# Two score banks become one tile of two halves, with 1024-column exponentials in the last slot of a gated two-branch attention kernel

## The chip, the cores and the metric

The kernel runs on one core of a Trainium2 chip. The metric is the device time of one execution in microseconds (us). Engines in what follows: TensorE (PE; its weight loads are PEld), VectorE (DVE), ScalarE (ACT), GpSimd (POOL) and SyncE (SP), which issues most DMAs.

## The reference

Two attention branches over the same 2048 x 512 input, 32 heads of 16 columns, are mixed by a gate per row:

```python
g = _sigmoid((x * gate_w).sum(-1, keepdims=True))
a = _A_ref(x, A_wq, A_wk, A_wv, A_wo, A_beta)
b = _B_ref(x, B_wqkv, B_wo)
return g * a + (1 - g) * b
```

Branch B is plain softmax attention over all 2048 positions: `p = softmax(q k^T / 4)`, `o = p v`, then `o @ wo`. Branch A splits the sequence into four segments of 512. Inside a segment it is causal softmax attention; the earlier segments come in through a memory state, `num / den` with `phi(q)` and `phi(k)`, weighted by `sigmoid(beta)` per head. All values are float32.

## The kernel before, in words

**Start** (to about 350 us). The input is transposed and split into a high and a low part (`do_x`), and the projections are made as three products of such parts: `v_job` (L255) for V and `qk_job` (L274) for Q and K, twelve matmuls of 512 columns each into one PSUM bank, which ScalarE copies out and, for Q and K, VectorE reads too. `mem_out`, `mem_put`, `mem_tr` and `mem_upd` (L304 to L359) make the memory branch of A. Each of these takes a bank from `misc()` (L95), which gives the least recently used of the banks in `mode["misc"]`.

**Slots** (L905 to L939). 32 slots follow, k = 0 to 31. A slot handles four heads and 512 query columns of B (unit 32 + k) and of A (unit k). It has NG = 37 groups: 32 of B (16 key tiles, two pairs of heads) and 5 of A (L489). For a group, in this order:
- `t_group` (L491) takes two banks, multiplies K with Q into them (two matmuls of 64 rows by 512 columns, side by side in the array; a group of A has up to four narrower ones), and ScalarE takes the exponential of each bank into SBUF (`raw`, L509). For A, GpSimd then masks the diagonal blocks (L512).
- the planned tasks: `s_b` (L442) or `s_a` (L417), products in the other orientation whose row maxima VectorE takes out of the two-bank tiles `sbk`; they serve the softmax of the next slot. `m_chain` and `m_rows` (L455, L472) bring the maxima into rows of Q.
- `pvs` (L826): `pv` (L515) multiplies the exponentials of an earlier key tile with V into the bank `pvb`, 256 columns at a time (512 in the last slot); `fin_copy` (L528) copies the result out.
- `out_mm` (L587), in one group of each slot from k = 9, is half of an output tile's projection.

Nothing reorders this: the order of the calls is the order on each engine. Waits are added by the framework from the tiles that an instruction reads and writes.

**PSUM** has eight banks of 512 columns: tb0 and tb1 (`TB`, L82), `pvb`, `mb`, and two tiles `sbk` of two banks each. In the slots `t_group`, `m_rows` and `out_mm` draw from `T3`, that is tb0, tb1 and mb (L821), least recently used first (`bank`, L88). In slot 31 there are no maxima for a next slot, and the first halves of the two `sbk` tiles join the rotation (L907), five banks in all.

**Planning.** `spread` (L892) puts the 32 `s_b` tasks of a slot at groups 20 to 31 and 36 of the slot before and at groups 1 to 19 of the slot itself; the six `s_a` tasks (`ST_A`, L637) go to groups 32 to 36 and to group 0 of the next slot (L902).

**End** (L940 to L967). The last four output tiles are projected into the banks `TAIL` (L822), copied out in halves and stored.

Of the kernel before, what the change touches and what calls it, by code (L numbers as in the profile page):

```python
# [7 lines left out]
FT = mybir.dt.float32  # L8
# [3 lines left out]
AF = mybir.ActivationFunctionType  # L12
# [9 lines left out]
C = 512  # L22
NC4 = SEQ // C
NT = SEQ // 128
SCALE = 0.25
MASK = -4.0e9
EARLY = 6
S_FIRST = 10
S_LAST = 10
# [4 lines left out]
def gated_mix_kernel(ctx, tc, x, wq, wk, wv, wo, beta, wqkv, wob, gate_w, out):  # L34
    nc = tc.nc
# [5 lines left out]
    PS = ctx.enter_context(tc.tile_pool(name="ps", bufs=1, space=PSUM))  # L41
# [19 lines left out]
    PTILE = [RAW[:, 4 * n:4 * n + 4] for n in range(2)]  # L61
# [17 lines left out]
    aux = P.tile([E, 2, 64], FT, name="aux")  # L79
    MST = [[X.tile([128, 8, 32], FT, name=f"mst{i}{s}") for s in range(2)] for i in range(2)]  # L80

    TB = [PS.tile([128, C], FT, name=f"tb{i}") for i in range(2)]  # L82
    PVB = PS.tile([128, C], FT, name="pvb")
    MB = PS.tile([128, C], FT, name="mb")
    SBK = [PS.tile([128, 2, C], FT, name=f"sbk{i}") for i in range(2)]
    lru = []

    def bank(allowed):  # L88
        b = min(allowed, key=lambda a: max([n for n, x in enumerate(lru) if x is a], default=-1))
        lru[:] = [x for x in lru if x is not b] + [b]  # L90
        return b

    mode = {"misc": TB + [MB, PVB] + [b[:, 0] for b in SBK]}

# [14 lines left out]
    def rot(key, lst):  # L109
        i = cnt.get(key, 0)  # L110
        cnt[key] = i + 1
        return lst[i % len(lst)]
# [262 lines left out]
    def q_of(u):  # L375
        return QA[u % 2] if u < 32 else QB[u % 3]

    def k_of(u, p):
        return KA[u % 2][:, p] if u < 32 else KB[(u - 32) % 3][:, p]

    def load_q(u):
        kd, qd, c = UN[u]
        load_qk(q_of(u), kd, 0, qd, c)

    def load_ka(u):
        kd, qd, c = UN[u]
        load_qk(KA[u % 2], kd, 1, qd, c)

    def load_kb(k, c=None):
        dst = KB[k % 3] if c is None else KB[k % 3][:, :, c * C:(c + 1) * C]  # L390
        load_qk(dst, "B", 1, k % 8, c)
# [63 lines left out]
    def m_chain(k):  # L455
        mx = pair_max(k)
        if k == 1:
            nc.vector.memset(mx[:, 0], 0.0)
        if k < 32:
            nc.vector.tensor_reduce(mx[:, 1], MXB.pop(32 + k).rearrange("q j p i c -> q (j p) i c"), axis=AX.X,  # L460
                                    op=OP.max)
        else:
            nc.vector.memset(mx[:, 1], 0.0)
        del MX[k]
        mx = mx.rearrange("q u h i -> q (u h i)")
        m8 = M8[k] = W.tile([128, 2, 32], FT, name="m8")
        hi = W.tile([128, 32], FR, name="mhi")
        nc.vector.tensor_scalar(hi, mx, -1.0, None, op0=OP.mult)
        nc.vector.tensor_copy(m8[:, 0], hi)
        nc.vector.scalar_tensor_tensor(m8[:, 1], mx, -1.0, hi, op0=OP.mult, op1=OP.subtract)  # L470
# [20 lines left out]
    def t_group(u, n, banks):  # L491


        kd, qd, c = UN[u]
        bs = [bank(banks) for _ in range(2)]
        c0 = 0
        for it, hs in (((n // 2, (n % 2 * 2, n % 2 * 2 + 1)),) if kd == "B" else GA[n]):
            q0 = 128 * it if kd == "A" else 0
            w = C - q0
            pn = it if kd == "B" else it % 2  # L500
            for j, h in enumerate(hs):
                r = slice(64 * j, 64 * j + 64)
                nc.tensor.matmul(bs[j][:, c0:c0 + w], k_of(u, h // 2)[r, 128 * it:128 * it + 128],  # L503
                                 q_of(u)[r, h // 2, q0:], start=True, stop=True)
                PT[u, it, h] = PTILE[pn % 2][:, 2 + j if (kd, it) == ("A", 2) else h][:, c0:c0 + w]
            c0 += w
        for j in range(2):
            pt = PTILE[pn % 2][:, 2 + j if (kd, n) == ("A", 4) else hs[j]]
            nc.scalar.activation(pt, bs[j], AF.Exp, scale=SCALE)  # L509
            if kd == "A":  # L510
                m = pt[:, :128] if n < 2 else pt.rearrange("p (a t) -> p a t", a=4)[:, ::3 if n < 4 else 2]
                nc.gpsimd.affine_select(out=m, in_=m, pattern=[[1, 128]] if n < 2 else [[0, 2], [1, 128]],  # L512
                                        compare_op=OP.is_ge, fill=0.0, base=0, channel_multiplier=-1)
# [14 lines left out]
    def fin_copy(u):  # L528

        ps = W.tile([128, C], FT, name="pvs", bufs=1)  # L530
        if u < 31:
            nc.vector.tensor_copy(ps, PVB)
        else:
            nc.scalar.activation(ps, PVB, AF.Copy)  # L534
        AT["pd", u] = D.tile([4, 32, C], FT, name=f"pd{u}")
        nc.sync.dma_start(AT["pd", u].rearrange("h r t -> (h r) t"), ps)
# [77 lines left out]
    def tail_mm(t, gs, a):  # L614
        op = tail_ops(t)
        for g in gs:
            for oi, wi in TERMS:
                nc.tensor.matmul(TAIL[t], op[oi][:, g, a], (AT["wh"], AT["wl"])[wi][:, g, a],
                                 start=(oi, wi, g, a) == (0, 0, 0, 0), stop=(oi, wi, g, a) == (1, 0, 3, 0))

    def tail_out(t):
        tt = 12 + t
        for hf in range(2):
            yo = RAW[:, t + 4 * hf, :256]
            h = slice(256 * hf, 256 * hf + 256)
            if hf:
                nc.scalar.activation(yo, TAIL[t][:, h], AF.Copy)
            else:
                nc.vector.tensor_copy(yo, TAIL[t][:, h])
            nc.sync.dma_start(outr[tt * 128:(tt + 1) * 128, h], yo)  # L630


    def todo(fn, *a):
        return lambda: fn(*a)
# [87 lines left out]
    for blk in range(16):  # L722
        g, c = divmod(blk, 4)
        pg, pc = divmod(blk - 1, 4)
        if blk == 4:
            mode["misc"] = TB + [MB, PVB]
        if 4 <= blk < 14:
# [5 lines left out]
        n = blk + 1 + (c == 2)  # L733
# [39 lines left out]
        for n in range(3):  # L773
# [8 lines left out]
            if nf == 35:  # L782
                mode["misc"] = [MB, PVB, TB[1]]
            if nf < want:
# [34 lines left out]
            set_aux(KB[2][:, p], 0)  # L819

    T3 = TB + [MB]  # L821
    TAIL = T3 + [SBK[0][:, 0]]  # L822
    mode["misc"] = T3
    NG = 2 * NT + 5

    def pvs(k, n):  # L826

        ua, ub = k, 32 + k
        if n == 0:
            if k:  # L830
                pv(ua - 1, 2)
                fin_copy(ua - 1)
        elif k == 31 and n < 2 * NT:
            if n % 2 and n > 1:
                pv(ub, n // 2 - 1)
        elif 2 <= n < 2 * NT + 2:
            pv(ub, n // 2 - 1, n % 2 * 256, n % 2 * 256 + 256)
            if n == 2 * NT + 1:
                fin_copy(ub)
        elif n > 2 * NT + 1:  # L840
            m = n - 2 * NT - 2
            if m < 2:
                pv(ua, 0, 256 * m, 256 * m + 256)
            else:
                pv(ua, 1)
                pv(ua, 3)
# [43 lines left out]
    plan = {}  # L890

    def spread(tasks, gs):  # L892
        for n, p in enumerate(gs):
            plan.setdefault(p, []).extend(tasks[len(tasks) * n // len(gs):len(tasks) * (n + 1) // len(gs)])

    for k in range(31):
        if k:
            spread([todo(s_b, 33 + k, *t) for t in (sorted(ST_B, key=lambda t: t[2]) if k == 1 else ST_B)],
                   [(k - 1, n) for n in list(range(2 * S_FIRST, 2 * NT)) + [NG - 1]] + [(k, n) for n in range(1, 2 * S_LAST)])
        else:  # L900
            spread(st33[EARLY:], sorted([(0, n) for n in range(2 * S_LAST)] + [(0, 2 * n) for n in range(4)]))
        for n, t in enumerate(ST_A):  # L902
            plan.setdefault((k, 2 * NT + n) if n < 5 else (k + 1, 0), []).append(todo(s_a, k + 1, *t))

    for k in range(32):  # L905
        ua, ub = k, 32 + k
        banks = T3 + [b[:, 0] for b in SBK] * (k == 31)  # L907
        for n in range(NG):
            it = n // 2 if n < NG - 1 else NT + 2
            t_group(*(ub, n) if n < 2 * NT else (ua, n - 2 * NT), banks)  # L910
            for f in plan.get((k, n), []) + ex[k][0].get(n, []):
                f()
            pvs(k, n)
            for f in ex[k][1].get(n, []):
                f()
            if n % 2 == 0 and n < NG - 1:
                continue
            beside(k, it)
            if it == S_LAST:
                m_chain(k + 1)  # L920
            if it == 4 and not k:
                late()
            if it == 4 and not k:
                load_q(ub + 2)
                for c in range(NC4):
                    load_kb(2, c)
            if it == NT and k < 29:
                load_q(ub + 3)
                load_kb(k + 3)
            if it == 6 and k < 31:  # L930
                load_q(ua + 1)
                load_ka(ua + 1)
                if (ua + 1) % 2 == 0:
                    load_va(ua + 1)
            if it == 9:
                if k % 2 == 0 and k < 30:
                    load_vb(k // 2 + 1)
                if 1 <= k <= 4:
                    load_wo(k - 1)  # L939
# [55 lines left out]
```

## Time and profile before

| | us |
|---|---|
| median of three runs | 1981.27 |
| lowest, highest | 1977.9, 1982.19 |
| span of the profiled execution, first to last instruction | 1976.0 |
| TensorE busy in it | 1944.8 |
| VectorE busy in it | 1630.3 |
| ScalarE busy in it | 1435.7 |

The profiled execution is a run of its own; what is known of its time is its span, which leaves out what lies before the first instruction and after the last. A row of the timeline gives the start and the duration in us, the engine, the line, the operation with what it writes and reads, and how many alike follow each other; in brackets stands the idle time of the engine before it and what ended it. A group's row of the page gives the count, the busy time in us, the mean in ns, and the idle time before. A row of the table of stages gives for one stretch its length, then the busy time and instructions of PE, PEld, DVE, ACT and POOL, the granted TensorE clock, the DMA share and GB/s. Ends of matmuls are modelled: what counts is from start to start.

### The profile page before, as it was taken

Reading aid. Unit: us, or ns where it says so; the run is one execution under the profiler, and the core shown is the slowest. Engines: PE = TensorE matmul, PEld = TensorE weight load, DVE = VectorE, ACT = ScalarE, POOL = GpSimd, SP = SyncE. Lnnn points to the kernel's source line nnn. Section 1 sums busy time; section 2 is a strip of 40 time slices with the busy share of each in tenths; the row PEclk is TensorE's granted clock in tenths of the full one; section 3 lists DMA queues with packets and bytes.
Section 4 is the critical chain, followed back from the end, with each engine's and each line's share of the span. In section 5 each row is a group of like instructions: output and inputs, shape, how many; then the busy total and the mean of one; then the engine's idle time right before and its main releaser. Section 6 shows DMA issues by size and latency. Waiting matters only on the chain.

```text
span 1976.0 us, 43643 instructions
## 1 busy us (share of the span) xinstructions
PE 1944.8 (98%) x17517; PEld 945.6 (48%) x17517; DVE 1630.3 (83%) x1825; ACT 1435.7 (73%) x2703; POOL 257.5 (13%) x474
## 2 busy tenths in 40 slices
PE   8999999999999999999999999999999999999999
PEld 6887777434344344444444444444444444444435
DVE  6135665899999999999999999999999999999942
ACT  3233332688888888888888888888888888888884
POOL 2200000011210101111010101010101010101012
PEclk9999999999999999999999999999999999999999
DMA  6766656644443444344445353444344444444111
GB/s 205 172 209 183 191 186 173 152 111 114 97 114 88 103 86 103 86 114 86 114 85 112 86 113 86 114 86 114 86 108 91 96 102 87 102 90 103 48 51 57
DMA packets 162742, 222.49 MB, mean 113 GB/s; under 512 B 39260, under 2 KB 89452, under 8 KB 156780
## 3 DMA queue, kind: packets, MB, share of 16 engines
q1 hardware_dynamic: 159596, 211.70, 44.0%
q0 software_dynamic: 2944, 8.00, 2.1%
q8 instruction: 138, 2.26, 0.5%
q14 instruction: 64, 0.52, 0.1%
HBM read 148.21 MB, written 68.16 MB: 109 GB/s over the span
## 4 chain that ended last, share of the span: by engine, by line
PE 90%; DMA 3%; DVE 2%; ACT 2%; issue 1%; SPq 1%; ACTq 0%; DVEq 0%
PE pvb L525 31%; PE tb L503 17%; PE sbk L449 12%; PE mb L503 8%; PE tb L279 3%; PE tb L591 2%; PE mb L279 2%; PE sbk L427 2%; PE pvb L279 2%; PE tb L262 2%; DVE mxb L451 1%; ACT raw L509 1%; PE mb L591 1%; PE mb L262 1%; PE sbk L431 1%
## 5 line engine op out<-in xcount | busy, mean ns | idle before, releaser
L451 DVE TENSOR_REDUCE mxb<-sbk 128x2 f32<-128x1024 f32 x1024 | 1226.1, 1222 | 36.6 <-PE sbk L449 32.4
L509 ACT ACTIVATE raw<-tb 128x512 f32<-128x512 f32 x1557 | 888.2, 598 | 163.1 <-PE tb L503 90.7
L525 PE MATMUL pvb<-raw,vb 128*17 128x256 f32 (+1 forms) x8072 | 639.4, 388 | 0.0
L509 ACT ACTIVATE raw<-mb 128x512 f32<-128x512 f32 x780 | 466.4, 598 | 76.5 <-PE tb L503 44.8
L503 PE MATMUL tb<-qb,xh 64*128 64x512 f32 x872 | 330.8, 496 | 1.7 <-ACT raw L509 1.7
L525 PEld LDWEIGHTS pvb<-raw,vb 128*17 128x17 f32 x8072 | 134.4, 95 | 341.7 <-issue 336.6
L449 PE MATMUL sbk<-xh,qb 64*128 64x512 f32 x1344 | 283.1, 398 | 2.0 <-DMA xh<-dB 0.8
L503 PE MATMUL mb<-qb,xh 64*128 64x512 f32 x445 | 219.6, 494 | 0.0
L503 PEld LDWEIGHTS tb<-qb,xh 64*128 64x128 f32 x872 | 124.4, 183 | 188.1 <-issue 91.4
L512 POOL TENSOR_SCALAR_AFFINE_SELECT raw<-raw 128x256 f32<-128x256 f32 (+1 forms) x320 | 116.1, 363 | 700.1 <-ACT raw L509 692.3
L503 PE MATMUL tb<-qb,kb 64*128 64x512 f32 x471 | 176.3, 496 | 1.4 <-DMA qb<-mr 0.8
L435 DVE TENSOR_REDUCE mx<-sbk 128x2 f32<-128x768 f32 (+1 forms) x128 | 139.8, 1092 | 43.1 <-PE sbk L431 37.1
L449 PE MATMUL sbk<-kb,qb 64*128 64x512 f32 x704 | 150.6, 406 | 1.2 <-DVE mxb L451 1.1
L449 PEld LDWEIGHTS sbk<-xh,qb 64*128 64x128 f32 x1344 | 137.9, 186 | 7.3 <-DVE mxb L451 3.5
L503 PEld LDWEIGHTS mb<-qb,xh 64*128 64x128 f32 x445 | 81.3, 183 | 86.6 <-issue 48.0
L503 PE MATMUL mb<-qb,kb 64*128 64x512 f32 x233 | 115.4, 495 | 0.7 <-DVE st L289 0.7
L565 POOL TENSOR_TENSOR o<-o,d 128x512 f32<-128x512 f32 x31 | 39.8, 1283 | 562.6 <-DMA d<-rd 281.6
L503 PEld LDWEIGHTS tb<-qb,kb 64*128 64x128 f32 x471 | 66.0, 183 | 98.4 <-issue 52.5
L525 PE MATMUL pvb<-raw,va 128*17 128x256 f32 (+2 forms) x1280 | 94.7, 383 | 5.8 <-ACT pvs L534 5.8
L427 PE MATMUL sbk<-ka,qa 64*128 64x256 f32 (+3 forms) x512 | 86.8, 346 | 1.2 <-ACT raw L509 1.2
L503 PE MATMUL tb<-qa,ka 64*128 64x384 f32 (+3 forms) x340 | 79.2, 372 | 0.0
L449 PEld LDWEIGHTS sbk<-kb,qb 64*128 64x128 f32 x704 | 71.6, 185 | 12.6 <-issue 6.5
(273 smaller groups left out, 1790.7 us busy)
## 6 DMA issues: line engine op xcount, KB each, us to landing
xh<-dB SPq DMA_DIRECT2D x38, 512.0 KB
vb<-vdB SPq DMA_DIRECT2D x16, 1088.0 KB
dB<-st SPq DMA_DIRECT2D x64, 256.0 KB
dA<-st SPq DMA_DIRECT2D x64, 256.0 KB
pd<-pvs SPq DMA_DIRECT2D x64, 256.0 KB
kb<-dB SPq DMA_DIRECT2D x22, 512.0 KB
xh<-dB SPq DMA_DIRECT2D x38, 256.0 KB
qb<-dB SPq DMA_DIRECT2D x64, 128.0 KB
```

Source lines behind the costliest of these rows:

```text
L262: nc.tensor.matmul(b, lhs, WV[wi][:, k, :], start=n == 0, stop=n == 11)
L279: nc.tensor.matmul(b, WS[ws][w][wi][:, k, :], (XH, XL)[xi][c][:, k, :], start=n == 0, stop=n == 11)
L427: nc.tensor.matmul(b[:, j, c0:c0 + n], q_of(u)[r, p, i * 128:(i + 1) * 128], k_of(u, p)[r, :n], start=True, stop=False)
L435: nc.vector.tensor_reduce(m[:, :, p, i], b[:, :, :n], axis=AX.X, op=OP.max)
L449: nc.tensor.matmul(b[:, j], q_of(u)[r, p, i * 128:(i + 1) * 128], k_of(u, p)[r, kc * C:(kc + 1) * C], start=True, stop=True)
L451: nc.vector.tensor_reduce(MXB[u][:, :, p, i, kc], b, axis=AX.X, op=OP.max)
L503: nc.tensor.matmul(bs[j][:, c0:c0 + w], k_of(u, h // 2)[r, 128 * it:128 * it + 128], q_of(u)[r, h // 2, q0:], start=True, stop=True)
L509: nc.scalar.activation(pt, bs[j], AF.Exp, scale=SCALE)
L512: nc.gpsimd.affine_select(out=m, in_=m, pattern=[[1, 128]] if n < 2 else [[0, 2], [1, 128]], compare_op=OP.is_ge, fill=0.0, base=0, channe ...
L525: nc.tensor.matmul(PVB[32 * h:32 * h + E + 1, q0 + lo:q0 + hi], vt[:, it, 4 * q + h, :], pt[:, lo:hi], start=it == 0 and lo == 0, stop=it ...
L565: nc.gpsimd.tensor_tensor(o, o, d, op=OP.mult)
L591: nc.tensor.matmul(b, (AT["oh"], AT["ol"])[oi][:, g, a], (AT["wh"], AT["wl"])[wi][:, g, a], start=n == 0, stop=n == 11)
```

## The change

- tb0 and tb1, two tiles, become one tile `tb` of two halves; `TB` is now the list of its halves.
- In the last slot, from group 2 on, `t_group` takes a whole two-bank tile in rotation (the two `sbk` tiles and `tb`), and one exponential of 1024 columns reads it. Groups 0 and 1 use T3. `misc()` gives mb alone there.
- A's last maxima tasks move up by one group: from groups 35, 36 and the next slot's 0 to 34, 35 and 36, in every slot. The `s_b` task of group 36 moves to group 0 of the next slot.
- The last `fin_copy` of branch B runs on VectorE in place of ScalarE.
- The four banks of the end are taken in the order mb, tb's halves, `sbk`.

```diff
-    TB = [PS.tile([128, C], FT, name=f"tb{i}") for i in range(2)]
+    tb = PS.tile([128, 2, C], FT, name="tb")
+    TB = [tb[:, i] for i in range(2)]
...
-        bs = [bank(banks) for _ in range(2)]
+        pair = None if banks else rot("pair", SBK + [tb])
+        bs = [pair[:, j] for j in range(2)] if pair is not None else [bank(banks) for _ in range(2)]
...
+        h0 = 2 if (kd, n) == ("A", 4) else hs[0]
+        if pair is not None:
+            nc.scalar.activation(PTILE[pn % 2][:, h0:h0 + 2], pair, AF.Exp, scale=SCALE)
         for j in range(2):
-            pt = PTILE[pn % 2][:, 2 + j if (kd, n) == ("A", 4) else hs[j]]
-            nc.scalar.activation(pt, bs[j], AF.Exp, scale=SCALE)
+            pt = PTILE[pn % 2][:, h0 + j]
+            if pair is None:
+                nc.scalar.activation(pt, bs[j], AF.Exp, scale=SCALE)
...
-        if u < 31:
+        if u < 31 or u == 63:
             nc.vector.tensor_copy(ps, PVB)
...
-    TAIL = T3 + [SBK[0][:, 0]]
+    TAIL = [MB, TB[0], TB[1], SBK[0][:, 0]]
...
-                   [(k - 1, n) for n in list(range(2 * S_FIRST, 2 * NT)) + [NG - 1]] + [(k, n) for n in range(1, 2 * S_LAST)])
+                   [(k - 1, n) for n in range(2 * S_FIRST, 2 * NT)] + [(k, n) for n in range(2 * S_LAST)])
...
-            plan.setdefault((k, 2 * NT + n) if n < 5 else (k + 1, 0), []).append(todo(s_a, k + 1, *t))
+            plan.setdefault((k, 2 * NT + n - (n > 2)), []).append(todo(s_a, k + 1, *t))
...
-        banks = T3 + [b[:, 0] for b in SBK] * (k == 31)
         for n in range(NG):
+            banks = T3 if k < 31 or n < 2 else None
+            if banks is None:
+                mode["misc"] = [MB]
```

## The prediction

> **What bounds the kernel now.** I read the page's busy times first, then the table of stages, then the timeline of the steady part.
>
> ```profile
> span 1976.0 us, 43643 instructions
> PE 1944.8 (98%) x17517; PEld 945.6 (48%) x17517; DVE 1630.3 (83%) x1825; ACT 1435.7 (73%) x2703; POOL 257.5 (13%) x474
> L451 DVE TENSOR_REDUCE mxb<-sbk 128x2 f32<-128x1024 f32 x1024 | 1226.1, 1222 | 36.6 <-PE sbk L449 32.4
> ```
> ```profile
> core 0: us, PE busy (x) PEld busy (x) DVE busy (x) ACT busy (x) POOL busy (x), PEclk, DMA share, GB/s
> 1200.00:1400.00 200.00, 199.36 (x1998) 84.69 (x1994) 184.37 (x190) 164.35 (x307) 25.97 (x46) 1.00 0.43 97
> ...
> 1950.00:1976.00 26.00, 22.15 (x95) 17.47 (x94) 10.25 (x26) 2.90 (x9) 5.30 (x9) 1.00 0.25 80
> ```
>
> In the steady stage TensorE is busy 199.4 us of 200, VectorE 184.4, ScalarE 164.4: three engines near their limits, TensorE nearest. A busy TensorE is modelled, so the instructions themselves have to say whether it has a gap:
>
> ```profile
> 1007.43 0.50 PE L503 MATMUL tb<-qb,xh 64*128 64x512 f32 x1
> ...
> 1007.43 0.49 PE L503 MATMUL mb<-qb,xh 64*128 64x512 f32 x1
> ...
> 1007.76 0.40 PE L449 MATMUL sbk<-xh,qb 64*128 64x512 f32 x2
> 1008.02 0.60 ACT L509 ACTIVATE raw<-tb 128x512 f32<-128x512 f32 x1 [0.20 <-PE tb L503]
> ...
> 1008.09 0.63 PE L525 MATMUL pvb<-raw,vb 128*17 128x256 f32 x8
> 1008.52 0.59 ACT L509 ACTIVATE raw<-mb 128x512 f32<-128x512 f32 x1
> ...
> 1008.65 0.52 PE L503 MATMUL tb<-qb,xh 64*128 64x512 f32 x2
> ```
>
> This is one group. The pair of score products starts at 1007.43, the maxima's products at 1007.76 (0.33 later), the products with V at 1008.09 (0.33), and the next pair at 1008.65 (0.56): 1.22 us, with TensorE issuing all the time. VectorE's reduction of one maxima task takes the same 1.222. No engine can give back a stall of TensorE here. The two exponentials start 0.59 and 1.09 after the pair and the second ends at 1009.11, **1.68 us after the pair**, 0.46 after the next pair has begun. That is harmless today: three banks rotate (tb0, tb1, mb), and a product waits only for the exponential that read its own bank three products earlier.
>
> **The change part by part.** *The merged tile.* The diff makes tb0 and tb1 one tile `tb` of two halves, in every stage and not just the last slot. I resolved the semaphore waits in the listing of the two built programs. Before, a product into tb0 waits for the exponential that read tb0. After, it waits for the last exponential that read `tb`, either half, and an exponential of a half waits for the last product into either half. 1,243 product waits of the changed program are for a reader of the other half. In the slots the three banks rotate through a cycle of three groups:
>
> ```
> group  products into   waits, after                              before
> a      tb half 0, 1    first exponential of group c (half 1)     own banks, three products back
> b      mb, tb half 0   tb: second exponential of group a         own banks, three products back
> c      tb half 1, mb   tb: second exponential of group b         own banks, three products back
> ```
>
> 305 whole cycles of this kind stand in the listing (305 waits with six matmuls between the writer and the wait, 608 with seven, 2 and 4 of them other products).
>
> What a hand-over from ScalarE to TensorE costs:
>
> ```profile
> 1911.00 0.62 ACT L509 ACTIVATE raw<-mb 128x512 f32<-128x512 f32 x1
> ...
> 1911.67 0.49 PE L503 MATMUL mb<-qb,xh 64*128 64x512 f32 x1
> ```
> ```profile
> 1044.19 0.60 ACT L534 ACTIVATE pvs<-pvb 128x512 f32<-128x512 f32 x1
> ...
> 1044.94 0.63 PE L525 MATMUL pvb<-raw,va 128*17 128x256 f32 x8 [0.16 <-ACT pvs L534]
> ```
>
> 0.05 us in the first (1911.62 to 1911.67, the same kind of product behind the same kind of exponential), 0.15 in the second (another kind, which waits for two semaphores). I take 0.06 and keep 0.15 for the range. With group a at 0:
> - a: exponentials 0.59 to 1.19 and 1.09 to 1.68.
> - b: mb's product goes at 1.22; tb's waits until 1.68 + 0.06 = 1.74, and the maxima and V products queue behind it. mb's exponential starts 1.22 + 0.59 = 1.81, tb's 1.74 + 0.59 = 2.33 and ends 2.93.
> - c: TensorE is free at 1.74 + 1.22 = 2.96; the wait ends 2.93 + 0.06 = 2.99. Its first exponential runs 3.58 to 4.18.
> - next a: TensorE free at 4.21, wait ends at **4.24**.
>
> Before, three groups took 3 x 1.22 = 3.66. So a cycle loses 0.58, almost all in b, and 305 cycles lose **177 us**. With 0.15 a hand-over the cycle is about 4.50 (0.84; 256 us); with b's stall alone, 0.52 (159 us). What queues behind the waiting product is all of TensorE's work, so VectorE waits too; DMAs have no part in it.
>
> *A's groups.* Five a slot, 155 in all. Their waits are alike, but A's maxima with their mask products lie between:
>
> ```profile
> 1042.63 0.49 PE L503 MATMUL tb<-qa,ka 64*128 64x512 f32 x1
> ...
> 1043.95 0.51 PE L503 MATMUL tb<-qa,ka 64*128 64x384 f32 x4
> ...
> 1045.50 0.44 PE L503 MATMUL mb<-qa,ka 64*128 64x384 f32 x1
> ```
>
> Pair to pair is 1.32 and 1.55, so a b stall is 0.42 or 0.19; a third of the groups, 52, at 0.3: **16 us** (10 to 22).
>
> *Row maxima (m_rows) and output products (out_mm).* They draw their bank from the same three.
>
> ```profile
> 980.67 0.50 PE L503 MATMUL mb<-qb,kb 64*128 64x512 f32 x1
> ...
> 981.81 0.39 PE L476 MATMUL tb<-ident,m 128*32 128x128 f32 x4
> 982.13 0.50 PE L503 MATMUL mb<-qb,kb 64*128 64x512 f32 x1
> 982.24 0.27 ACT L478 ACTIVATE mr<-tb 64x128 f32<-64x128 f32 x1
> ```
> ```profile
> 1050.45 0.50 PE L503 MATMUL mb<-qb,xh 64*128 64x512 f32 x1
> ...
> 1051.12 1.19 PE L591 MATMUL tb<-wh,oh 128*128 128x512 f32 x4
> ...
> 1054.05 0.18 PEld L503 LDWEIGHTS mb<-qb,xh 64*128 64x128 f32 x1 [0.35 <-issue]
> ...
> 1054.16 0.69 DVE L598 TENSOR_TENSOR yo<-tb,yo 128x512 f32<-128x512 f32 x1 [1.59 <-PE tb L591]
> ```
>
> In 23 of the slots m_rows now waits for the last exponential on `tb`: 1.74 after its pair in place of 1.14, 0.60 each. In 24 the next product waits for the copy of the maxima: 982.51 + 0.06 in place of 982.13, 0.44. Together 24 us. In 14 slots out_mm waits until 1.74 in place of 0.67 (1.07), and in 15 the next product for its result: 1054.85 + 0.06 in place of 1054.05 (0.86). Together 28 us, of which I take 25 since the pause lets ScalarE catch up. Sum **49 us**, half of it as the low end.
>
> *The projections at the start.* There the listing has 52 waits for the other half: 26 with nothing between, 14 with at most eight matmuls, 12 with more (free).
>
> ```profile
> 98.78 1.07 PE L262 MATMUL tb<-wv,xl 128*128 128x512 f32 x4
> 99.69 0.49 PE L336 MATMUL mb<-ident,phi 128*128 128x128 f32 x3
> 99.94 0.60 ACT L267 ACTIVATE vb<-tb 128x512 f32<-128x512 f32 x1 [1.98 <-PE tb L262]
> ```
>
> A job's last products start at 98.78, the next job at 99.69, and the copy out ends at 100.54: a job that must wait for the copy loses 0.91. 26 x 0.91 + 14 x 0.4 (an estimate, the middle of 0 and that) = **30 us** (15 to 45; jobs that VectorE reads too wait longer, those at the very start may be hidden by loads).
>
> *The last slot*, the change's name. ScalarE bounds it:
>
> ```profile
> 1927.93 0.83 ACT L509 ACTIVATE raw<-mb 128x512 f32<-128x512 f32 x1
> ...
> 1930.37 0.84 ACT L509 ACTIVATE raw<-mb 128x512 f32<-128x512 f32 x1
> ```
> ```profile
> 1902.47 1.06 ACT L584 ACTIVATE oh<-o 128x1024 fp32r<-128x1024 f32 x1
> ```
>
> Five exponentials in 2.44, 0.49 each in a stream, 0.98 a group. No 1024-column exponential from PSUM is in the trace. The nearest row is the 1024-column copy from SBUF, 1.06 alone; less the 0.11 by which streamed exponentials overlap (0.60 - 0.49), 0.95. So 0.03 a group saved; if all of the 0.11 went, 0.11. Over 35 groups 1 to 4 us; I take **3**, with a copy (fin_copy of 63) that leaves ScalarE. The Trainium skill, "ScalarE: Activation LUTs", section "What ACT_TABLE_LOAD costs", gives 186 ns + 0.833 ns a column with immediate operands and an overlap of 93 ns back to back; an estimate from it is 93 ns saved a pair, 3.3 us. The trace's 0.49 stands beside its 0.52 for 512 columns.
>
> *At nothing:* A's last maxima tasks one group earlier, and one B task from the last group to the next slot's first. The same instructions run, TensorE has no gap on either side, and the orders of SP and POOL do not change, so no DMA is issued past another. Without that cover VectorE's gaps at the slot's end bound it:
>
> ```profile
> 1046.38 0.96 DVE L435 TENSOR_REDUCE mx<-sbk 128x2 f32<-128x768 f32 x1 [0.59 <-PE sbk L431]
> ...
> 1047.88 1.23 DVE L437 TENSOR_REDUCE mx<-sbk 128x4 f32<-128x1024 f32 x1 [0.55 <-PE sbk L431]
> ```
>
> One such gap, 0.55 in 31 slots, is 17 us either way. The order of the final banks changes nothing before the last copies.
>
> **Sum:** 177 + 16 + 49 + 30 - 3 = 269 us. 1976.0 + 269 = 2245; the median of the runs, 1981.27, stands 5.3 above this span, so **2250 us**.
>
> **Rivals.**
> 1. *The halves stay apart in effect*: the added waits are over when the product comes, and only the last slot changes. It decides if the second exponential ended less than 1.16 after its pair; the rows say 1.68. Then 1981 - 3 = 1978, and with one of VectorE's gaps closed by the moved tasks (17 us) 1961, **faster**. The Trainium skill, "PSUM — Partial Sum Buffer", section "PSUM bank collisions raise a hardware error", asks for semaphores by bank and quadrant: by it the chip would allow the halves to be apart, as the two-tile program's trace shows with tb0 and tb1 in use side by side. The listing has the waits all the same. Chance 0.03.
> 2. *Part of the stall is absorbed*: the product into mb runs ahead, ScalarE catches up, and only half of each loss stays: 1981 + 135 = 2116; 2060 to 2180. For it: mb's early product does start its exponential early. Against: tb's exponential sets the next wait, and the cycle above has that in it. Chance 0.12.
> 3. *Dearer hand-overs*: 0.15 at each of three links, and longer waits in the projections: 256 + 22 + 49 + 45 - 3 = 369, 2350; 2310 to 2400. For it: the second row. Chance 0.2.
> 4. *The clock drops* as TensorE idles. The Trainium skill, "TensorE: Matmul & The Clock Gate", section "Why this matters for your kernels", warns of idle gaps over some 3 us. As a mechanism here: granted 1.00 at 22.15 busy of 26 (85%), the share that 2250 would give, and the new gaps are 0.5. A drop to half would add some hundreds of us, above 2400. Chance 0.02.
>
> **How the numbers follow.** The forecast, 2250 with its own 2180 to 2310, has 0.63. The range that leaves out 0.2: **2170 to 2350**, which holds the forecast, the bound of 0.15 a hand-over and the upper part of rival 2. 0.2% (4 us) is what a measurement of this kernel can tell from no change: faster 0.02, same 0.01, slower 0.97.
>
> **What would show it.** Right: pair to pair in three steps near 1.74, 1.25, 1.25 where all were 1.22; TensorE's idle time released by exponentials, some 0.5 a cycle; VectorE's share falling to about 73%; the last slot alone shorter by 1 to 4 us; the granted clock still 1.00. Wrong: pairs still 1.22 apart (rival 1), or the long step well under 1.6 (rival 2). Two things would upset the sum: a hand-over that is not 0.06, and false waits in the projections that other waits already cover.

## The result, and the profile after

The changed kernel takes 2226.93 us, median of five runs (2225.28 to 2231.9), where the kernel before takes 1981.65 (five runs): a ratio of 1.1245, 95% interval 1.1225 to 1.1265. It is slower, by 245 us. The forecast was 2250, range 2170 to 2350.

The page of the changed kernel, whose line numbers are one to six higher than before (L505 is L503, L515 is L509, L452 is L451):

```profile
span 2223.5 us, 43972 instructions
PE 2113.2 (95%) x17517; PEld 994.5 (45%) x17517; DVE 1657.3 (75%) x1826; ACT 1443.8 (65%) x2667; POOL 257.1 (12%) x474
L452 DVE TENSOR_REDUCE mxb<-sbk 128x2 f32<-128x1024 f32 x1024 | 1245.2, 1225 | 208.4 <-PE sbk L450 200.9
```

All three engines fell in share though their work is all but the same: the sign of a wait, not of an operation. VectorE's idle time before its maxima rose from 36.6 to 208.4 us, and TensorE's products released it: it starves behind TensorE. What TensorE itself waits for shows the score products' line, first before and then after (idle time in us, times):

```profile
  issue: 247.9, 602
  ACT raw L509: 236.1, 558
```
```profile
  ACT raw L515: 517.6, 1268
  issue: 101.9, 230
```

Idle time until an exponential rose from 236 to 518 us (the weight loads' idle time is in both). One full cycle of the three groups, in the timeline of the changed kernel:

```profile
1101.57 0.50 PE L505 MATMUL tb<-qb,kb 64*128 64x512 f32 x1
1101.57 0.49 PE L505 MATMUL mb<-qb,kb 64*128 64x512 f32 x1
...
1102.79 0.50 PE L505 MATMUL tb<-qb,kb 64*128 64x512 f32 x2
...
1103.38 1.09 ACT L515 ACTIVATE raw<-tb 128x512 f32<-128x512 f32 x2 [0.20 <-PE tb L505]
...
1104.31 0.50 PE L505 MATMUL mb<-qb,kb 64*128 64x512 f32 x1
1104.52 0.50 PE L505 MATMUL tb<-qb,kb 64*128 64x512 f32 x1
...
1106.05 0.50 PE L505 MATMUL tb<-qb,kb 64*128 64x512 f32 x1 [0.24 <-ACT raw L515]
```

Group a starts at 1102.79. Its exponentials run 1103.38 to 1104.47, and b's product into `tb` goes 0.05 later, at 1104.52: **1.73 after the pair**, where every step was 1.22. The maxima and V products behind it move with it. The next step here, 1.53 to 1106.05, is one of the longer ones, because `mb`'s product of b, at 1104.31, was 0.3 late; of 231 steps from b to c only 24 were over 1.3. Counted over the trace from 800 us to the last slot (some 230 steps of each kind between groups that follow each other), the medians are 1.74 from a to b, 1.22 from b to c and 1.22 from c to a; the means 1.734, 1.249 and 1.225. Before, the means were 1.240, 1.239, 1.239. A cycle loses 0.49.

Where the 247.5 us between the two spans lie, by marks in both traces (the first score product, and the copies of the row maxima, one a slot):

| stretch | before | after | more |
|---|---|---|---|
| start to the first score product | 349.3 | 401.6 | 52.3 |
| to the maxima copy of slot 0 | 46.4 | 52.1 | 5.7 |
| 30 slots, copy to copy | 1491.8 | 1679.4 | 187.6 |
| from there to the end, with the last slot | 88.5 | 90.4 | 1.9 |

From copy to copy, a slot without output products went from 48.1 to 53.8 in the mean, one with them from 50.3 to 56.8: 55.9 in one of three, 57.1 or 57.4 in the others, as `out_mm` draws mb or a half of `tb`.

The stage table shows the same, with the clock (after, then before, the first stretch of each being the start):

```profile
0.00:401.60 401.60, 345.24 (x1585) 262.34 (x1585) 181.57 (x310) 113.42 (x234) 36.33 (x71) 0.98 0.57 163
...
1200.00:1400.00 200.00, 195.38 (x1768) 78.95 (x1764) 166.97 (x172) 148.97 (x275) 23.33 (x38) 1.00 0.36 84
```
```profile
0.00:349.30 349.30, 334.69 (x1585) 259.06 (x1585) 180.35 (x310) 112.12 (x234) 36.32 (x71) 0.99 0.65 188
```

The start has the same 1585 matmuls in both, but TensorE lies idle 56 us instead of 15. In 200 us of the steady stage 1768 matmuls run where 1998 did; the granted clock is 1.00.

### The profile page after: what moved, and what is told of

It reads as the page before. It is cut to its first block, busy times and chain, and to the rows that moved or that the text cites. A ratio compares the mean times of both kernels' runs of the same rounds, so it can differ in the third digit from the quotient of the medians.

```text
span 2223.5 us, 43972 instructions
## 1 busy us (share of the span) xinstructions
PE 2113.2 (95%) x17517; PEld 994.5 (45%) x17517; DVE 1657.3 (75%) x1826; ACT 1443.8 (65%) x2667; POOL 257.1 (12%) x474
## 4 chain that ended last, share of the span: by engine, by line
PE 76%; ACT 5%; DVE 2%; issue 2%; DMA 1%; SPq 0%; POOL 0%; ACTq 0%; DVEq 0%
PE pvb L531 27%; PE tb L505 22%; PE sbk L450 10%; PE mb L505 7%; ACT raw L515 4%; PE sbk L428 2%; PE tb L597 2%; PE sbk L432 1%; PE mb L597 1%; PE tb L280 1%; PE mb L280 1%; DVE mxb L452 1%; PE tb L624 1%; PE sbk L505 0%; DMA dB<-st 0%
## 5 line engine op out<-in xcount | busy, mean ns | idle before, releaser
L452 DVE TENSOR_REDUCE mxb<-sbk 128x2 f32<-128x1024 f32 x1024 | 1245.2, 1225 | 208.4 <-PE sbk L450 200.9
L515 ACT ACTIVATE raw<-tb 128x512 f32<-128x512 f32 x1530 | 871.3, 595 | 348.4 <-PE mb L505 182.4
L515 ACT ACTIVATE raw<-mb 128x512 f32<-128x512 f32 x768 | 456.9, 595 | 65.2 <-PE mb L505 21.1
L505 PE MATMUL tb<-qb,xh 64*128 64x512 f32 x869 | 324.0, 495 | 28.0 <-ACT raw L515 10.9
L450 PE MATMUL sbk<-xh,qb 64*128 64x512 f32 x1344 | 334.6, 410 | 0.8 <-DVE mxb L452 0.5
L505 PEld LDWEIGHTS tb<-qb,xh 64*128 64x128 f32 x869 | 119.9, 183 | 274.0 <-ACT raw L515 248.2
L505 PE MATMUL mb<-qb,xh 64*128 64x512 f32 x435 | 215.4, 495 | 0.0
L505 PE MATMUL tb<-qb,kb 64*128 64x512 f32 x471 | 175.5, 498 | 12.1 <-DMA qb<-mr 3.2
L450 PE MATMUL sbk<-kb,qb 64*128 64x512 f32 x704 | 176.1, 417 | 0.6 <-DVE mxb L452 0.6
L450 PEld LDWEIGHTS sbk<-xh,qb 64*128 64x128 f32 x1344 | 150.7, 186 | 5.8 <-DVE mxb L452 2.8
L505 PEld LDWEIGHTS tb<-qb,kb 64*128 64x128 f32 x471 | 64.8, 183 | 144.3 <-ACT raw L515 131.0
L505 PEld LDWEIGHTS mb<-qb,xh 64*128 64x128 f32 x435 | 79.5, 183 | 84.3 <-issue 46.1
L505 PE MATMUL mb<-qb,kb 64*128 64x512 f32 x233 | 115.5, 496 | 0.8 <-DVE st L290 0.8
L428 PE MATMUL sbk<-ka,qa 64*128 64x256 f32 (+3 forms) x512 | 97.2, 361 | 0.1
L450 PEld LDWEIGHTS sbk<-kb,qb 64*128 64x128 f32 x704 | 78.0, 186 | 11.8 <-issue 7.5
L505 PE MATMUL tb<-qa,ka 64*128 64x512 f32 (+3 forms) x338 | 77.9, 372 | 1.3
```

Source lines behind the costliest of these rows:

```text
L428: nc.tensor.matmul(b[:, j, c0:c0 + n], q_of(u)[r, p, i * 128:(i + 1) * 128], k_of(u, p)[r, :n], start=True, stop=False)
L450: nc.tensor.matmul(b[:, j], q_of(u)[r, p, i * 128:(i + 1) * 128], k_of(u, p)[r, kc * C:(kc + 1) * C], start=True, stop=True)
L452: nc.vector.tensor_reduce(MXB[u][:, :, p, i, kc], b, axis=AX.X, op=OP.max)
```

## The experiments

**Theory:** the waits on the other half of `tb` are the whole loss. **Rivals:** the moved tasks or the paired last slot carry a part; or the loss has to do with something other than the chain of exponentials, such as where the banks lie. Each ratio is against runs of the kernel before on the same chip.

**The merged tile alone.**

```diff
-    TB = [PS.tile([128, C], FT, name=f"tb{i}") for i in range(2)]
+    tb = PS.tile([128, 2, C], FT, name="tb")
+    TB = [tb[:, i] for i in range(2)]
```

> The kernel before with one edit: tb0 and tb1 are one tile of two halves. My theory (the added waits on the other half are the whole loss): 2228, the changed kernel's 2227 plus the 1.3 us that its paired exponentials won, within 4. Rival (the moved tasks or the paired last slot carry a part): 1982 to 2150. The pair-to-pair steps of the slots would be 1.74, 1.22, 1.22 by my theory and 1.22 three times by the rival.

Measured 2245.17, ratio 1.1326 (1.131 to 1.1341), with steps of 1.74, 1.22, 1.22. The mechanism stands, the number was 17 too low. Its span is 20.0 above the changed kernel's, and by the marks 13.8 of this lie from the last slots' mark to the end (104.2 against 90.4) and 6.3 in the 30 slots (56.19 a slot against 55.98; in those slots only the moved tasks differ between the two kernels, and how they would save 0.2 a slot was not followed). I had forgotten that in this kernel the halves rotate as single banks in the last slot too. Its timeline there:

```profile
2173.80 0.50 PE L504 MATMUL mb<-qb,xh 64*128 64x512 f32 x1
2173.81 0.50 PE L504 MATMUL tb<-qb,xh 64*128 64x512 f32 x1
...
2175.03 0.69 ACT L510 ACTIVATE raw<-tb 128x512 f32<-128x512 f32 x1
2175.77 0.49 PE L504 MATMUL tb<-qb,xh 64*128 64x512 f32 x1 [1.46 <-ACT raw L510]
```

The product at 2175.77 goes 0.05 after the exponential of the other half ends at 2175.72. So the paired reading, which takes both halves at once and lets no half wait for the other, spares the changed kernel most of these 14 us, which its own merging would have cost: 12.0 of them lie behind the slot's second pair of score products.

**tb0 and tb1 apart, all else as in the changed kernel.**

```diff
-    tb = PS.tile([128, 2, C], FT, name="tb")
-    TB = [tb[:, i] for i in range(2)]
+    TB = [PS.tile([128, C], FT, name=f"tb{i}") for i in range(2)]
...
-        pair = None if banks else rot("pair", SBK + [tb])
-        bs = [pair[:, j] for j in range(2)] if pair is not None else [bank(banks) for _ in range(2)]
+        pair = None if banks else rot("pair", SBK + [TB])
+        bs = TB if pair is TB else [pair[:, j] for j in range(2)] if pair is not None else [bank(banks) for _ in range(2)]
+        pair = None if pair is TB else pair
```

> The changed kernel with tb0 and tb1 as two tiles again; in the last slot the two sbk tiles are still read by one 1024-column exponential each, tb0 and tb1 by two of 512. My theory: 1980, that is 1981.7 less about 1.5 (0.06 for two pairs in three, over 35 groups), 1976 to 1982. Rival (the rest of the change costs too): over 1990.

Measured 1979.02, ratio 0.9979 (0.9968 to 0.999); the steps are 1.22 three times. The whole loss is gone with the one tile. That rules out the rest of the change as a cause of it.

**The moved tasks alone** (the last two hunks of `plan` in the kernel before).

```diff
-        [... range(2 * S_FIRST, 2 * NT)) + [NG - 1]] + [(k, n) for n in range(1, 2 * S_LAST)])
+        [... range(2 * S_FIRST, 2 * NT)] + [(k, n) for n in range(2 * S_LAST)])
...
-            plan.setdefault((k, 2 * NT + n) if n < 5 else (k + 1, 0), [])...
+            plan.setdefault((k, 2 * NT + n - (n > 2)), [])...
```

> The kernel before with the moved tasks alone (A's last maxima tasks one group earlier, one B task from group 36 to the next slot's group 0). My theory: 1981.7 within 4, since TensorE has no gap on either side of the move. Rival (VectorE's gaps at the slot's end count): 0.55 a slot less or more, 1964 or 1999.

Measured 1979.66, ratio 0.9981 (0.9972 to 0.9989): a gain of 2 to 6 us, at the edge of what I had allowed. A slot stays at 49.71 against 49.73, so VectorE's gaps did not count. In its one profiled run the gain lies in the last slot: from the mark to the end 86.8 against 88.5. Before, the first group of that slot held a task of A in an `sbk` tile that the score products wanted as well. First the kernel before, then this one:

```profile
1903.25 0.50 PE L503 MATMUL sbk<-qb,xh 64*128 64x512 f32 x2 [0.34 <-DVE mx L437]
...
1904.92 0.33 PE L427 MATMUL sbk<-ka,qa 64*128 64x128 f32 x2 [1.17 <-ACT raw L509]
...
1906.09 0.50 PE L503 MATMUL mb<-qb,xh 64*128 64x512 f32 x1
```
```profile
1905.84 0.50 PE L503 MATMUL sbk<-qb,xh 64*128 64x512 f32 x2
...
1906.83 0.50 PE L503 MATMUL mb<-qb,xh 64*128 64x512 f32 x1
```

From the first pair of the slot to the second 2.84 us before, 0.99 with the task gone: 1.85. From the mark to that second pair, with the task now ahead of the slot, 1.8 are left of it.

**The paired last slot alone** (tb0 and tb1 apart, tasks where they were).

```diff
+        pair = None if banks else rot("pair", SBK + [TB])
...
+        if pair is not None:
+            nc.scalar.activation(PTILE[pn % 2][:, h0:h0 + 2], pair, AF.Exp, scale=SCALE)
```

> The kernel before with the paired last slot alone, tb0 and tb1 apart, no moved tasks. My theory: 1980, 1976 to 1982, the same as with the moved tasks. Rival (the two parts need each other): differs from the run with both by over 4.

Measured 1977.35, ratio 0.9976 (0.9966 to 0.9987). It gives no less than both parts together; its interval and those of the two runs above overlap, so what the parts add to each other can't be told. Besides the paired exponentials it holds the other edits to the last slot and the end: `fin_copy` on VectorE, the order of the final banks, and T3 for groups 0 and 1. These two groups no longer draw on `sbk`, so the conflict just shown is gone here too: 1.39 us from the first pair to the second (mb at 1905.19, tb at 1906.58), with the task still between them.

**Shorter exponentials, with the merged tile and without.**

```diff
-            nc.scalar.activation(pt, bs[j], AF.Exp, scale=SCALE)
+            cut = 256 if kd == "B" and u < 63 and j else C
+            nc.scalar.activation(pt[:, :cut], bs[j][:, :cut], AF.Exp, scale=SCALE)
```

> The kernel before with the merged tile, and in the slots before the last the second exponential of each of B's groups covers 256 of its 512 columns (the other half is left out, so the output is not the reference's). My theory: the step from a group in both halves to the next is the two exponentials' end plus a hand-over, so it falls by the shortening, from 1.74 to about 1.53 (a 256-column copy took 0.39 where 512 took 0.60), and 305 cycles give 64 us: about 2164 if the merged tile alone gives 2228. Rival (the loss has to do with where the banks lie or with something else than the chain of exponentials): the same time as the merged tile alone, 2228.

> The kernel before, tb0 and tb1 apart, with the same shortened second exponentials (their other 256 columns left out). My theory: ScalarE is not the bound there, 1981 within 5. Rival (shorter exponentials help whatever the tile): as much less as the merged tile gains from them, 1917 if that is 64.

With the merged tile 2173.95, ratio 1.0973 (1.0946 to 1.1): 71 below the merged tile alone, where 64 was expected and 0 by the rival. Apart 1975.95, ratio 0.9966 (0.9951 to 0.998): 7 less, just outside the 5 that were allowed, and 64 by its rival. The step from a to b in the first of them:

```profile
1121.71 0.50 PE L504 MATMUL tb<-qb,xh 64*128 64x512 f32 x2
...
1122.32 0.87 ACT L511 ACTIVATE raw<-tb 128x512 f32<-128x512 f32 x2 [0.42 <-PE tb L504]
...
1123.24 0.49 PE L504 MATMUL tb<-qb,xh 64*128 64x512 f32 x1
```

1.53 instead of 1.74, and 0.05 after the exponentials' end at 1123.19. The second exponential took 0.38 instead of 0.59 and the step fell by as much: the chain product, two exponentials, product sets it. Where the tiles are apart the same shortening moves almost nothing.

**Merged only from the slots on.** The start keeps two tiles, whose pool is closed ahead of the slots.

```diff
+    early_tb = ExitStack()
+    PT0 = early_tb.enter_context(tc.tile_pool(name="ps0", bufs=1, space=PSUM))
+    TB = [PT0.tile([128, C], FT, name=f"tb{i}") for i in range(2)]
...
+    early_tb.close()
+    PT1 = ctx.enter_context(tc.tile_pool(name="ps1", bufs=1, space=PSUM))
+    tb = PT1.tile([128, 2, C], FT, name="tb")
+    TB = [tb[:, i] for i in range(2)]
```

> The changed kernel, but tb0 and tb1 are two tiles until the slots begin and become one tile of two halves there. My theory: the stage before the slots loses nothing and the slots lose what they lose in the changed kernel, so 2227 - 52 = 2175, within 5, with the first score product at about 350 us. Rival (the start's delay is made up later, since what it delays is needed only in the slots): 2227.

Measured 2178.7, ratio 1.0996 (1.0971 to 1.1021), 48 less than the changed kernel. The first score product comes at 349.6 as before, and a slot takes 56.02 as in the changed kernel. So the start's loss is a loss of its own and nothing makes it up later.

**Merged only in the last slot**, from its group 2, in the same way; with the moved tasks and without them.

> The changed kernel with tb0 and tb1 as two tiles until group 2 of the last slot, where their place becomes one tile of two halves; so all that the last slot does is as in the changed kernel, and nothing is merged where single banks rotate. My theory: all of the loss goes, and a third of the pairs (12 of 35) win their 0.06 each beside the version with tb apart: 1978, 1975 to 1982, ratio to before 0.997 to 0.999. Rival (the last slot or the end pay for the merged tile too, through its two halves as final banks): 1981 or more.

> The same without the moved tasks. My theory: 1978, within 2 of the version with them, since either the moved tasks or the paired last slot alone took 0.2% and both together no more. Rival (the moved tasks add to the pairs): 4 more than the version with them.

Measured 1978.03, ratio 0.9975 (0.9963 to 0.9988), and 1977.08, ratio 0.9967 (0.9956 to 0.9978). Both beat the kernel before, by 0.1 to 0.4%. So all that the change does from group 2 of its last slot on can be had without the loss; the loss is in the places where the halves rotate as single banks. Between these two and the two versions with separate tiles nothing can be told. What the gain is due to shows when the time from the last slots' mark on is cut at the slot's second pair of score products (us, one profiled run each):

| kernel | mark to the second pair | from there to the end |
|---|---|---|
| before | 18.6 | 69.9 |
| moved tasks alone | 16.8 | 70.0 |
| paired last slot alone, tiles apart | 16.7 | 68.9 |
| all but the merging | 16.8 | 69.4 |
| merged in the last slot, with the moved tasks | 16.8 | 70.3 |
| merged in the last slot, without them | 16.7 | 69.9 |
| changed | 19.8 | 70.6 |

The first column gains 1.8 in every version without the early merging: the conflict for `sbk` is gone in all of them. The second column, where the pairs are, gains nothing with the joint tile, and 0.6 to 1.0 with the tiles apart. So no gain from 1024-column exponentials on the joint tile is shown. By the medians these five versions gain 4 to 6 us; the cut places 1.5 to 2.8 of it, and where the rest lies stays open (the profiled run of the kernel before is the fastest of its five, and the mean granted clock of the runs differed a little, 0.997 before and 0.997 to 0.998 here).

## Why the prediction was right, point by point

- **The mechanism held.** The added waits came from the listing of the built program, and the trace shows them where the three-group cycle put them: 1.74 at b, with a hand-over of 0.05 in 301 of 302 such steps (0.06 was taken). Shortening the exponential shortened that step by the same amount, and separate tiles removed it.
- **The cycle's other two steps were mis-sized**: 1.25 each was forecast, and their medians are 1.22, TensorE's own work. The exponential behind b's late product starts sooner than the 0.59 that the cycle took: 0.53 or 0.54 after it in 144 of 302 steps, 0.56 or 0.57 in 137. In the changed kernel:

```profile
1100.35 0.50 PE L505 MATMUL tb<-qb,kb 64*128 64x512 f32 x1
...
1100.88 0.60 ACT L515 ACTIVATE raw<-tb 128x512 f32<-128x512 f32 x1
1101.01 0.63 PE L531 MATMUL pvb<-raw,vb 128*17 128x256 f32 x8
...
1101.57 0.50 PE L505 MATMUL tb<-qb,kb 64*128 64x512 f32 x1
```

  The exponential starts 0.53 after the late product and not 0.59, so it ends 1.13 after it, and the next product goes at 1.22. At 0.57 too, with 0.60 for the exponential and 0.05 for the hand-over, the wait is over at 1.22. 305 cycles at 0.49 (by the means) are 149 us; 177 was the term.
- **A's groups, m_rows and out_mm**: 65 us forecast. A slot without `out_mm` lost 5.7, of which 9.8 cycles (305 in 31 slots) explain 4.8. What is left for A's groups and `m_rows`, which were not measured apart, is about 0.9 a slot, 27 in all against 40. With `out_mm` a slot lost 6.5, some 0.8 more, 18 in 23 slots against 25.
- **The start was mis-sized the other way**: 52 us measured, 48 by the experiment, 30 forecast (15 to 45). The count of waits is that of the listing, which no run checks; the price was that of one projection's copy, 0.91, for all that have nothing between, and the trace has dearer ones. Matched product by product with the trace of before, `mem_out` (L311) lost 12.0 us, `v_job` 14.2 and `qk_job` 15.0. Two rows of the changed kernel show why some waits are dearer:

```profile
72.48 0.60 ACT L268 ACTIVATE vb<-tb 128x512 f32<-128x512 f32 x1 [0.96 <-DMA vdA<-vb]
73.13 2.17 PEld L263 LDWEIGHTS tb<-wv,xh 128*128 128x128 f32 x7 [4.28 <-ACT vb L268]
```
```profile
125.81 0.73 PE L312 MATMUL tb<-mst,phi 128*128 128x136 f32 x4 [1.81 <-ACT om L315]
```

  In the first the copy that the product waits for waits itself for a store to give its buffer back, and a slack in DMA became a stall of TensorE of some 4 us. In the second, two products of one `mem_out` that ran as one row before (1.10 at 106.62) are parted by two copies that stand behind two other operations of ScalarE.
- **The last slot**: forecast 3 less, by its paired exponentials. The changed kernel gained nothing there: of its 1.9 more from the mark on, about 2.1 belong to the 12 groups left of slot 30 (12/37 of 6.5). The 85.7 from the mark to the end of the paired slot with separate tiles, against 88.5, bear the forecast out in the number alone: 1.85 of these 2.8 are the conflict for `sbk`, which the forecast did not have. In the changed kernel the first two groups still rotate the halves, and the output products wait there; behind the second pair it took 70.6, no less than the 69.9 before, though the pairs follow each other faster where they stream. Where the slot loses that again was not followed. A row from the first groups' end, and the stream:

```profile
2154.14 1.20 PE L597 MATMUL tb<-wh,oh 128*128 128x512 f32 x4 [0.74 <-ACT raw L515]
...
2164.93 1.12 ACT L511 ACTIVATE raw<-tb 128x1024 f32<-128x1024 f32 x1
...
2165.85 2.04 ACT L511 ACTIVATE raw<-sbk 128x1024 f32<-128x1024 f32 x2
...
2167.68 1.12 ACT L511 ACTIVATE raw<-tb 128x1024 f32<-128x1024 f32 x1
```

  Three pairs in 2.75, 0.92 each, where 0.98 was the time of two single ones and 0.95 was taken. Over some two dozen pairs that stream this would be 1.5 us, an estimate that no stretch above shows as a gain with the joint tile. The estimate from the Trainium skill's page "ScalarE: Activation LUTs" (section "What ACT_TABLE_LOAD costs"), 0.093 a pair, is more than the 0.06 of these rows.
- **The moved tasks**, costed at nothing, do nothing in a slot of the kernel before; they win some 1.8 us once, in the last slot of the kernel before, where they end a conflict for an `sbk` tile that I did not look for.
- **Rivals.** The halves are not apart in effect (1.74, not 1.22). The stall is not half absorbed (the cycle kept 0.49 of the 0.58). The hand-overs were not dearer: in the 302 steps from a to b 0.05, and once 0.13. The clock did not fall: 1.00 in the steady stage, although TensorE idles there.

The terms afterwards: 149 + 27 + 18 + 52 + 0 = 246, against 247.5 between the spans; since 27 and 18 are what was left over, this is no check of them. The forecast's sum of 269 was 23 above that by errors of opposite sign: the cycle 28 and the smaller users of the banks 20 too dear, the start 22 and the last slot 3 too cheap. That it came within 1% of the time is in part luck.

## What to carry to other kernels

Before joining two buffers to let one instruction read both, list who still uses them singly: where dependencies are kept by tile, each half then waits for the other's readers, in every stage that uses the tile, not just in the one that the change is for. Read the waits in the built program, then write down one full cycle of the rotation with start-to-start times; an engine that was full loses the whole stall. The joint view can be made where it is used, by closing the small tiles and opening the large one in their place: the last two runs do so and lose nothing. That the joint view itself gains is not shown, so look at what a gain comes from before putting it down to the edit that was meant to bring it.

## What the runs showed of the hardware

An exponential's end reached the waiting matmul in 0.05 us in 301 of 302 steps of the changed kernel, and in 0.13 in the other. A product whose partner had run ahead had its exponential start 0.53 to 0.57 after it in most steps, instead of 0.59; why was not tried. A 1024-column exponential out of PSUM took 1.02 us where ScalarE had been idle before it (five such, 1024 or 1025 ns), and 0.92 from start to start in a stream, where two of 512 columns take 0.98.
